# Attention beside an MLP on one core: small transfers on GpSimd's queue, the output weights' norm in the first stage, and six steps instead of four before heads' results are read

## The chip, the core and the metric

The kernel runs on one core of a Trainium2 chip. The metric is the device time of one execution in microseconds (us), the median of several runs. The engines are named as in the profile: PE (TensorE's matmuls), PEld (its weight loads), DVE (VectorE), ACT (ScalarE), POOL (GpSimd), SP (the engine that issues most transfers).

## The reference

For x of 2048 rows and 640 columns, with 32 heads of 20 columns and an MLP of width 1536:

```python
xn = _layernorm(x, axis=-1)
return x + _A_ref(xn, A_wqkv, A_wo) + _B_ref(xn, B_w1, B_b1, B_w2, B_b2)

# _A_ref(x, wqkv, wo): q, k, v = x @ wqkv, by head
scores = jnp.einsum("bhqd,bhkd->bhqk", q, k) * (Dh ** -0.5)
p = _softmax(scores, axis=-1)
o = jnp.einsum("bhqk,bhkd->bhqd", p, v)
return o (heads side by side) @ wo

# _B_ref(x, w1, b1, w2, b2)
y = _layernorm(x, axis=-1)
h = _gelu(y @ w1 + b1)
return h @ w2 + b2
```

## The kernel before

Numbers that need float32 are carried as pairs of 16-bit halves, and most products are three matmuls of halves. So that the halves keep their precision, each weight matrix is scaled by a power of two taken from its sum of squares: `squares` or a loop of ScalarE's Square activations, then `pow2` (one small matmul against ones into a PSUM tile of the tag "s", and a few VectorE operations on one column), then `split` (ScalarE scales into a tile of the tag "wtmp", VectorE casts the high half and subtracts for the low one).

**First stage (up to about 220 us).** Four chunks `c` of 512 rows. For each, `norm_a`, `norm_b` and `norm_c` make the layer norm (the reciprocal roots are powers on POOL), five steps `qk(c, tt)` make q and k for all heads, and `qk_out` stores them in DRAM (`qkscr`) in halves; then four steps `vproj(c, j)` make V, and `vproj_out` puts it in the tile `vfull`. Between these steps `some(n)` advances the generator `weights()`, which takes the sums of squares of w2 and w1 and then splits w2 (12 slices) and w1 (15 slices). PSUM has three tiles of the tag "s" in turn for qk, vproj and the norms' small matmuls. `norm_c` stores the second norm's 512 reciprocals per chunk as 4-byte elements in DRAM (`rscr`, line 272); lines 537 and 538 store a constant row and load the bias b1 (1536 elements of 4 bytes). All of these transfers are issued by SP.

**Attention (about 220 to 1281 us).** 16 pairs of heads `g`, two halves `hf` of the query rows, two column blocks `cc` and 16 key blocks `kb`, in groups of four key blocks; for the pairs below TAIL = 12 the halves alternate, after that all of half 0 comes before half 1. Each key block gives two score matmuls (`scores`, line 711), an exp on ScalarE (line 713) and, for half of the blocks, a subtraction `low` on VectorE (line 725); `pv` multiplies with V (line 742). Into these groups `other()` puts the MLP's matmuls (`layer1`, `layer2`, then `projection`) at a fixed rate. The order of everything is written out by the program: `tick()` is called twice per group and advances each side generator by one step. Generators in `sides` advance at every step; those in `patient` only in a step in which nothing else gave VectorE work, unless their last step was a mere wait.

**Finishing.** After three (later two) pairs of a half, `finish` is queued in `fins`, and one runner (`finishing`) works them off: it loads the sums of exps, takes reciprocals, stores them (`linv`), loads them back spread over the heads' rows (`rb`) and loads the two partial results (`oa` from `opart`), waits a number of steps, adds, multiplies, splits into halves and stores to `oscr` (lines 889 to 899), for 512 columns at a time. The runner was put into `sides` when it was created for half 1 at pair TAIL or later, else into `patient`.

**Output weights.** `prep_late` (line 658) starts when the MLP's first layer has ended: it loads wo over w1's place, waits four steps, squares its five slices on ScalarE one step each, takes `pow2`, and splits them on VectorE. The projection with wo comes last, half of it after attention.

Of the kernel before, what the change touches and what calls it, by code (L numbers as in the profile page):

```python
# [16 lines left out]
P = 128  # L17
# [25 lines left out]
def mha_mlp_kernel(tc, x, wqkv, wo, w1, b1, w2, b2, out):  # L43
# [4 lines left out]
    with (  # L48
# [53 lines left out]
        def pow2(acc, tag):  # L102

            lo = keep.tile([P, 1], F32, name=f"lo_{tag}")
            hi = keep.tile([P, 1], F32, name=f"hi_{tag}")
            if tag in ("q", "k"):
                pt = psM.tile([P, 512], F32, tag="m", name="mxp")
            else:
                pt = psS.tile([P, 2, 512], F32, tag="s", name="mxp")[:, 0, :]
            n = acc.shape[1]  # L110
            nc.tensor.matmul(pt[:, :n], ones, acc, start=True, stop=True)
            nc.vector.tensor_reduce(lo, pt[:, :n], AX.X, ALU.add)  # L112
# [10 lines left out]
        def split(pool, src, h, l, scale, n):  # L123

            tmp = pool.tile([P, n], F32, tag="wtmp", name="wtmp")
            nc.scalar.activation(tmp, src, AF.Copy, scale=scale)
            nc.vector.tensor_copy(h, tmp)
            nc.vector.tensor_sub(l, tmp, h)
# [33 lines left out]
        with tc.tile_pool(name="pa", bufs=2) as pa, tc.tile_pool(name="pa1", bufs=1) as pa1, tc.manual_schedule():  # L162
# [106 lines left out]
            def norm_c(c):  # L269
                mv, ve, r, r2 = rs.pop(c)  # L270
                newton(r2, ve, "b")
                nc.sync.dma_start(rscr[c * 512 : (c + 1) * 512].rearrange("(j p) -> p j", p=P), r2)

            xnts = {}

# [181 lines left out]
            def weights():  # L457

                for i in range(KF // 2):
                    if i == 0:  # L460
                        accs["2"] = sm.tile([P, 8], F32, tag="acc2", name="acc2", bufs=1)[:, : KF // 2]
                    nc.scalar.activation(junk[:, : 2 * D].rearrange("p (a b) -> p a b", a=2),
                                         w2t[:, 2 * i : 2 * i + 2, :], AF.Square, accum_out=accs["2"][:, i : i + 1])
                    yield
                scale_of("2")
                yield
                for k in range(KD):
                    if k == 0:
                        accs["1"] = sm.tile([P, 8], F32, tag="acc1", name="acc1", bufs=1)[:, :KD]
                    nc.scalar.activation(junk[:, :F], w1t[:, k, :], AF.Square, accum_out=accs["1"][:, k : k + 1])  # L470
                    yield
                scale_of("1")
                yield
                factors()
                yield
                for k in range(KF):
                    split(pa, w2t[:, k, :], w2v[:, k, 0], w2v[:, k, 1], scales["2"], D)
                    yield
                for k in range(KD):
                    for q in range(3):  # L480
                        split(pa, w1t[:, k, q * 512 : (q + 1) * 512], w1v[:, k, q, 0], w1v[:, k, q, 1], scales["1"], 512)
                        yield
# [51 lines left out]
                split_qkv("q", [k], 0, 2 * P)  # L534
            nc.sync.dma_start(xscr[:, :, :, :512], xnts[0])
            del xts[0]
            nc.sync.dma_start(bscr[H : H + 1, :].rearrange("h (r t) -> h r t", r=4), brow[0:1, None, :].to_broadcast([1, 4, S // 4]))
            nc.sync.dma_start(b1t, b1.rearrange("(k p) -> p k", p=P))
            for c in range(4):
                nxt = c + 1 if c < 3 else None  # L540
                for tt in range(5):
# [76 lines left out]
        with ExitStack() as scope:  # L618
# [36 lines left out]

            split_done = []

            def prep_late(tag, w, wv_, src, nk, slices, delay):
                nc.sync.dma_start(w, src)
                for _ in range(delay):  # L660
                    yield
                acc = sm.tile([P, 8], F32, tag="acc", name="acc")
                for i, sl in enumerate(slices):
                    junk = m1.tile([P, 2 * MC], F32, tag="u", name="junk").bitcast(BF16)[:, :D]
                    nc.scalar.activation(junk, w[:, sl, :], AF.Square, accum_out=acc[:, i : i + 1])
                    yield
                yield
                yield
                pw[tag] = pow2(acc[:, : len(slices)], tag)
                s = keep.tile([P, 1], F32, name=f"s_{tag}")  # L670
                nc.vector.tensor_scalar(s, pw[tag][1], 4096.0, None, ALU.mult)
                nc.vector.tensor_scalar(fo, pw["v"][0], 2.0**-22, pw[tag][0], ALU.mult, ALU.mult)
                yield 1.0
                for k in range(nk):
                    parts = []
                    for tag_, c0 in (("u", 0), ("w", 320)):
                        tmp = m1.tile([P, 2 * MC], F32, tag=tag_, name="wtmp")[:, :320]
                        nc.vector.tensor_scalar(tmp, w[:, k, c0 : c0 + 320], s, None, ALU.mult)
# [6 lines left out]
                split_done.append(tag)  # L685

            def project(ot, acc, t0, j):
                for hf in range(2):
# [82 lines left out]
            def unload(g, hf, ev):  # L771
                cols = slice(hf * 1024, (hf + 1) * 1024)
                direct.extend([ev] if (g, hf) == ORDER[-1] else [])
                for p in range(0 if direct else 2):
                    dma(g, hf)(lpart[p, hf, 2 * g : 2 * g + 2, :].rearrange("a (c t) -> a c t", c=2),
                                      ev[PAD + DH + VW * p :: 64])
                    for a in range(2):
                        q0, r = 64 * a + PAD + VW * p, (2 * g + a) * DH
                        dma(g, hf)(opart[p, r : r + DH, cols].rearrange("d (c t) -> d c t", c=2),
                                          ev[q0 : q0 + DH])  # L780
                if g + 1 in ENDS:
                    fins.append(finish(g + 1 - UNITS[ENDS.index(g + 1)], g + 1, hf))
                    if len(fins) == 1:

                        (sides if hf == 1 and g + 1 >= TAIL else patient).append(finishing())

            def waits(n):
                for _ in range(n - 1):
                    yield WAIT
                yield  # L790

            fins, direct = [], []
            ready = [0, 0]

            fetched = []
# [24 lines left out]
            def finish(g0, g1, hf):  # L820
# [16 lines left out]
                for c0 in range(0, 1024, w):  # L837
# [50 lines left out]
                    for h in range(0 if last else nh):  # L888
                        go(rb[h * DH : (h + 1) * DH],
                           linv[hf, 2 * g0 + h : 2 * g0 + h + 1, c0 : c0 + w].to_broadcast([DH, w]))  # L890
                    yield from waits(W2 if last else 4)
                    nc.vector.tensor_add(o0, o0, o1)
                    yield
                    nc.vector.tensor_mul(o0, o0, rb)
# [64 lines left out]
            def layer1(mc, f):  # L959
                xnt, r2f = xs[mc]  # L960
                if f == 0:
                    hTs[mc] = m0.tile([P, KF, 2, MC], F16, tag="hT", name="hT")
                ps = psM.tile([P, 2, MC], F32, tag="m", name="pu")
                for i in range(2):
                    n = 0
                    fo_ = (f + i) % 4 * P
                    for k in range(KD):
                        for a, b in PASS:
                            nc.tensor.matmul(ps[:, i], w1v[:, k, (f + i) // 4, a, fo_ : fo_ + P], xnt[:, k, b, :],  # L969
                                             start=(n == 0), stop=(n == 3 * KD - 1))  # L970
                            n += 1
                            if n % 3 == 0:
                                if i == 1 and n == 15:
                                    begin(gelu(ps, r2f, hTs[mc], f))
                                    over[0] = True
                                yield 0.3276
                if f == KF - 2:
                    if mc + 2 < NMC:
                        load_chunk(mc + 2)
                    if mc + 1 == NMC:  # L980
                        sides.append(ahead())
                        sides.append(prep_late("o", wot, wov, wo.rearrange("(k p) n -> p k n", p=P), KD,
                                               range(KD), 4))

            xbs = {}

# [292 lines left out]
```

## Time and profile before

| what | value |
|---|---|
| median of 3 runs | 1352.96 us (1352.85 to 1353.47) |
| the profiled execution's own time | 1354.35 us |
| its span, first to last instruction | 1352.6 us |
| granted TensorE clock | 0.998 |
| busy | PE 98%, ACT 83%, DVE 78%, PEld 44%, POOL 2% of the span |
| bytes moved by DMA | 127.94 MB, 95 GB/s on average |

A timeline row gives the start, the length, the engine, the line and operation, the tiles written and read, how many instructions are merged, and in brackets the idle time before it and what ended that. A row of the groups has busy time and mean length of one instruction, then the idle time before the group. In the chain of waits each piece has its start, length and what it was.

### The profile page before, as it was taken

What the parts mean: (1) busy time and instruction counts of PE and PEld (TensorE: products, weight loads), DVE (VectorE), ACT (ScalarE), POOL (GpSimd) and SP (SyncE); (2) the same over time, 40 slices, a digit from 0 to 9 for tenths busy, and PEclk for the clock granted to TensorE, in tenths of its full rate; (3) what the DMA queues carried; (4) which work ended last, traced back from release to release, by engine and by line L of the source; (5) the groups of instructions that cost most, each with busy time, mean ns of one, the idle gap of its engine ahead of it and who ended that gap; (6) DMA issues with size and microseconds to landing.
All of it is one profiled execution on the core that took longest, in us unless ns stands there. A gap on an engine that the chain in (4) does not pass through costs nothing.

```text
span 1352.6 us, 29045 instructions
## 1 busy us (share of the span) xinstructions
PE 1331.5 (98%) x11647; PEld 591.7 (44%) x11647; DVE 1056.0 (78%) x1436; ACT 1128.2 (83%) x1306; POOL 30.0 (2%) x74
## 2 busy tenths in 40 slices
PE   9999999999999999999999999999999999999997
PEld 6545545443334343434434343443433333333475
DVE  6658735998779887978897789887888898878732
ACT  7754425999999999999999999999999999999800
POOL 2000000000000000000000000000000000000000
PEclk9999999999999999999999999999999999999999
DMA  9976632121123231123321142313032323153375
GB/s 271 250 200 142 141 102 58 34 55 40 48 69 89 65 85 56 49 57 86 97 67 53 28 110 57 92 48 86 19 99 74 100 57 87 54 171 83 102 222 178
DMA packets 103217, 127.94 MB, mean 95 GB/s; under 512 B 27660, under 2 KB 69712, under 8 KB 103076
## 3 DMA queue, kind: packets, MB, share of 16 engines
q1 hardware_dynamic: 100324, 120.27, 31.6%
q0 software_dynamic: 2304, 5.24, 2.3%
q8 instruction: 93, 1.52, 0.5%
q10 hardware_dynamic: 448, 0.51, 0.2%
q14 instruction: 48, 0.39, 0.1%
HBM read 80.50 MB, written 42.51 MB: 91 GB/s over the span
## 4 chain that ended last, share of the span: by engine, by line
PE 80%; DVE 7%; ACT 6%; DMA 4%; issue 2%; SPq 1%; DVEq 0%; ACTq 0%; POOL 0%; POOLq 0%
PE o L742 25%; PE s L711 16%; PE py L1001 10%; PE pu L969 9%; PE qkp L323 8%; PE z L1080 5%; PE vp L396 5%; ACT p L713 4%; DVE low L725 3%; DMA w1t<-in_A_wo_dram 1%; DMA qkscr<-qkhl 1%; PE warm L220 1%; DMA accscr<-xb 0%; DMA oa<-opart 0%; DVE u L906 0%
## 5 line engine op out<-in xcount | busy, mean ns | idle before, releaser
L713 ACT ACTIVATE p<-s 128x1024 f32<-128x1024 f32 x1024 | 971.6, 1044 | 41.3 <-PE s L711 35.5
L725 DVE TENSOR_TENSOR low<-p 128x1024 f16<-128x1024 f32 x512 | 614.3, 1218 | 155.1 <-ACT p L713 154.8
L742 PE MATMUL o<-p,vfull 128*32 128x512 bf16 (+1 forms) x4096 | 429.7, 493 | 0.0
L711 PE MATMUL s<-qs,ks 61*128 61x512 f16 x2048 | 316.4, 381 | 8.3 <-ACT p L713 7.3
L711 PEld LDWEIGHTS <-ks 61*128 61x128 f16 x2048 | 63.6, 94 | 294.6 <-issue 291.0
L969 PE MATMUL pu<-xm,w1t 128*128 128x256 f16 x1440 | 179.3, 273 | 1.4 <-DVE u L906 1.4
L1001 PE MATMUL py<-w2t,hT 128*128 128x320 f16 x1152 | 178.4, 300 | 1.6 <-DVE u L906 1.5
L969 PEld LDWEIGHTS <-w1t 128*128 128x128 f16 x1440 | 130.6, 98 | 68.7 <-issue 55.3
L1001 PEld LDWEIGHTS <-hT 128*128 128x128 f16 x1152 | 102.6, 98 | 88.7 <-issue 54.5
L323 PE MATMUL qkp<-xnt,wv 128*128 128x512 f16 x600 | 131.1, 379 | 1.2 <-DVE lo_v L112 0.9
L742 PEld LDWEIGHTS <-vfull 128*32 128x32 f16 x3072 | 59.5, 95 | 132.4 <-issue 101.8
L742 PE MATMUL o<-low,vfull 128*32 128x512 f16 x1024 | 102.2, 378 | 0.2
L323 PEld LDWEIGHTS <-wv 128*128 128x128 f16 x600 | 58.3, 98 | 71.0 <-DVE wv L430 1.1
L742 PEld LDWEIGHTS o<-p,vfull 128*32 128x32 f32 x2048 | 62.5, 108 | 53.1
L338 ACT ACTIVATE qkhl<-qkp,qks 128x1024 f16<-128x1024 f32 (+1 forms) x24 | 23.3, 969 | 64.4 <-PE qkp L323 47.3
L396 PE MATMUL vp<-wv,xnt 128*128 128x320 f16 x480 | 66.7, 299 | 0.0
L1080 PE MATMUL z<-w1t,ot 128*128 128x320 f16 x480 | 66.3, 299 | 0.0
L339 DVE SCALAR_TENSOR_TENSOR qkhl<-qkp,qks,qkhl 128x1024 f16<-128x1024 f32 (+1 forms) x24 | 26.5, 1106 | 37.9 <-ACT qkhl L338 37.8
L1080 PEld LDWEIGHTS <-ot 128*128 128x128 f16 x480 | 46.5, 98 | 20.8 <-issue 2.9
L396 PEld LDWEIGHTS <-xnt 128*128 128x128 f16 x480 | 46.7, 98 | 18.6
L1039 DVE SCALAR_TENSOR_TENSOR acc<-z,sc,acc 128x320 f32<-128x320 f32 x32 | 17.4, 546 | 42.8 <-PE z L1080 37.0
L763 ACT ACTIVATE ev<-o 128x512 f32<-128x512 f32 x64 | 39.3, 615 | 2.5 <-PE o L742 2.5
(182 smaller groups left out, 666.6 us busy)
## 6 DMA issues: line engine op xcount, KB each, us to landing
qkscr<-qkhl SPq DMA_DIRECT2D x40, 256.0 KB
opart<-ev SPq DMA_DIRECT2D x124, 80.0 KB
ks<-qkscr SPq DMA_DIRECT2D x120, 80.0 KB
qs<-qkscr SPq DMA_DIRECT2D x192, 40.0 KB
oa<-opart SPq DMA_DIRECT2D x32, 240.0 KB
xt<-in_A_x_dram SPq DMA_DIRECT2D x16, 320.0 KB
xscr<-xnt SPq DMA_DIRECT2D x4, 1280.0 KB
xm<-xscr SPq DMA_DIRECT2D x8, 640.0 KB
```

Of the source, the lines that this page charges most:

```text
L323: nc.tensor.matmul(ps[:, i, :], wv[:, k, q, a, mm * P : (mm + 1) * P], xnts[c][:, k, b, :], start=(k + n == 0), stop=(k == KD - 1 and n == 2))
L338: nc.scalar.activation(hl[:, 0, i0:i1], ps[:, i0:i1], AF.Copy, scale=a)
L339: nc.vector.scalar_tensor_tensor(hl[:, 1, i0:i1], ps[:, i0:i1], a, hl[:, 0, i0:i1], ALU.mult, ALU.subtract)
L396: nc.tensor.matmul(ps[:, hf, :320], xnts[c][:, k, a, j * P : (j + 1) * P], wv[:, k, 2, b, hf * 320 : (hf + 1) * 320], start=(n == 0), stop ...
L711: nc.tensor.matmul(ps[:, a, :], ks[64 * a : 64 * a + 61, kb * P : (kb + 1) * P], qs[64 * a : 64 * a + 61, cc * 512 : (cc + 1) * 512], star ...
L713: nc.scalar.activation(pt, ps, AF.Exp, scale=QS)
L725: nc.vector.tensor_sub(low, pt, upper(pt))
L742: nc.tensor.matmul(pv.o[32 * q : 32 * q + 32, :], src[:, v0 - PAD * (1 - q % 2) :][:, :32], t, start=q not in pv.begun, stop=last, skip_gr ...
L763: nc.scalar.activation(evs[g, hf][:, cc], pv.o, AF.Copy)
L969: nc.tensor.matmul(ps[:, i], w1v[:, k, (f + i) // 4, a, fo_ : fo_ + P], xnt[:, k, b, :], start=(n == 0), stop=(n == 3 * KD - 1))
L1001: nc.tensor.matmul(ps[:, :320], hTs[mc][:, f, a, j * P : (j + 1) * P], w2v[:, f, b, hf * 320 : (hf + 1) * 320], start=(n == 0), stop=(n == ...
L1080: nc.tensor.matmul(ps[:, :320], ot[:, k, a, j * P : (j + 1) * P], wov[:, k, b, h * 320 : (h + 1) * 320], start=(n == 0), stop=(n == 3 * KD ...
```

## The change

The small transfers (`rscr`, the constant row of `bscr`, b1) are issued by POOL instead of SP. The sums of squares of wo are taken in the first stage: between the splits of w2, POOL loads one 128 x 640 slice at a time into a tile of the tag "wtmp" and ScalarE squares it two splits later; the scale and the output's factor `fo` are made among w1's splits. `prep_late` keeps the load of wo, now waits eight steps, and goes straight to the splits. `finish` waits six steps instead of four before adding, except for the last two units of each half, which keep four. Its runner always begins in `patient` and moves to `sides` once a half-1 unit beyond pair 12 has been queued.

```diff
@@ norm_c
-                nc.sync.dma_start(rscr[c * 512 : (c + 1) * 512].rearrange("(j p) -> p j", p=P), r2)
+                nc.gpsimd.dma_start(rscr[c * 512 : (c + 1) * 512].rearrange("(j p) -> p j", p=P), r2)
@@ weights
+                accs["o"] = sm.tile([P, 8], F32, tag="acco", name="acco", bufs=1)[:, :KD]
+                came = []
                 for k in range(KF):
+                    if k % 2 == 0 and 0 < k <= 2 * KD:
+                        nc.scalar.activation(junk[:, :D], came[-1], AF.Square, accum_out=accs["o"][:, k // 2 - 1 : k // 2])
                     split(pa, w2t[:, k, :], w2v[:, k, 0], w2v[:, k, 1], scales["2"], D)
+                    if k % 2 == 0 and len(came) < KD:
+                        came.append(pa.tile([P, D], F32, tag="wtmp", name="wos"))
+                        nc.gpsimd.dma_start(came[-1], wo[k // 2 * P : (k // 2 + 1) * P, :])
                     yield
                 for k in range(KD):
+                    if k == 1:
+                        scale_of("o")
+                        nc.vector.tensor_scalar(fo, pw["v"][0], 2.0**-22, pw["o"][0], ALU.mult, ALU.mult)
                     for q in range(3):
@@ first stage
-            nc.sync.dma_start(bscr[H : H + 1, :].rearrange("h (r t) -> h r t", r=4), brow[0:1, None, :].to_broadcast([1, 4, S // 4]))
-            nc.sync.dma_start(b1t, b1.rearrange("(k p) -> p k", p=P))
+            nc.gpsimd.dma_start(bscr[H : H + 1, :].rearrange("h (r t) -> h r t", r=4), brow[0:1, None, :].to_broadcast([1, 4, S // 4]))
+            nc.gpsimd.dma_start(b1t, b1.rearrange("(k p) -> p k", p=P))
@@ prep_late
-            def prep_late(tag, w, wv_, src, nk, slices, delay):
+            def prep_late(w, wv_, src, nk, delay):
                 nc.sync.dma_start(w, src)
-                for _ in range(delay):
-                    yield
-                acc = sm.tile([P, 8], F32, tag="acc", name="acc")
-                for i, sl in enumerate(slices):
-                    junk = m1.tile([P, 2 * MC], F32, tag="u", name="junk").bitcast(BF16)[:, :D]
-                    nc.scalar.activation(junk, w[:, sl, :], AF.Square, accum_out=acc[:, i : i + 1])
-                    yield
-                yield
-                yield
-                pw[tag] = pow2(acc[:, : len(slices)], tag)
-                s = keep.tile([P, 1], F32, name=f"s_{tag}")
-                nc.vector.tensor_scalar(s, pw[tag][1], 4096.0, None, ALU.mult)
-                nc.vector.tensor_scalar(fo, pw["v"][0], 2.0**-22, pw[tag][0], ALU.mult, ALU.mult)
-                yield 1.0
+                yield from waits(delay)
                 for k in range(nk):
...
@@ unload
                     if len(fins) == 1:
-                        (sides if hf == 1 and g + 1 >= TAIL else patient).append(finishing())
+                        patient.append(finishing())
+                        runner[:] = patient[-1:]
+                    if hf == 1 and g + 1 > TAIL and runner[0] not in sides:
+                        patient.remove(runner[0])
+                        sides.append(runner[0])
@@ finish
-                    yield from waits(W2 if last else 4)
+                    yield from waits(W2 if last else 4 if g1 > TAIL else 6)
@@ layer1
-                        sides.append(prep_late("o", wot, wov, wo.rearrange("(k p) n -> p k n", p=P), KD,
-                                               range(KD), 4))
+                        sides.append(prep_late(wot, wov, wo.rearrange("(k p) n -> p k n", p=P), KD, 8))
```

More of the change, by code (lines that the diff above doesn't have):

```diff
@@ L677, in prep_late @@
                         tmp = m1.tile([P, 2 * MC], F32, tag=tag_, name="wtmp")[:, :320]
-                        nc.vector.tensor_scalar(tmp, w[:, k, c0 : c0 + 320], s, None, ALU.mult)
+                        nc.vector.tensor_scalar(tmp, w[:, k, c0 : c0 + 320], scales["o"], None, ALU.mult)
                         parts.append((tmp, slice(c0, c0 + 320)))
@@ L684, in prep_late @@
                         yield 0.7
-                split_done.append(tag)
+                split_done.append(1)
             def project(ot, acc, t0, j):
@@ L790, in waits @@
                 yield
-            fins, direct = [], []
+            fins, direct, runner = [], [], []
             ready = [0, 0]
```

## The prediction

> **What bounds the kernel now.** I read the page's totals first, then a table of 30 us stretches, and then the rows of TensorE's timeline that show a pause.
>
> ```profile
> PE 1331.5 (98%) x11647; PEld 591.7 (44%) x11647; DVE 1056.0 (78%) x1436; ACT 1128.2 (83%) x1306; POOL 30.0 (2%) x74
> L713 ACT ACTIVATE p<-s 128x1024 f32<-128x1024 f32 x1024 | 971.6, 1044 | 41.3 <-PE s L711 35.5
> L725 DVE TENSOR_TENSOR low<-p 128x1024 f16<-128x1024 f32 x512 | 614.3, 1218 | 155.1 <-ACT p L713 154.8
> 1060.00:1090.00 30.00, 28.21 (x269) 11.55 (x267) 26.80 (x33) 27.84 (x33) 0.85 (x1) 1.00 0.35 91
> 1090.00:1120.00 30.00, 29.17 (x270) 11.73 (x270) 26.34 (x35) 28.37 (x33) 0.00 (x0) 1.00 0.19 52
> 1150.00:1180.00 30.00, 29.91 (x286) 11.78 (x287) 23.69 (x31) 29.23 (x34) 0.00 (x0) 1.00 0.19 56
> 1210.00:1240.00 30.00, 27.03 (x238) 10.42 (x234) 20.07 (x36) 28.66 (x38) 0.00 (x0) 1.00 0.32 99
> ```
>
> In a stretch row the columns after the length are busy us (and instructions) of PE, its weight loads, DVE, ACT and POOL, then clock, DMA share and GB/s. TensorE is busy 98% of the span at full clock. ScalarE's exps wait 41.3 us, 35.5 of them for TensorE's scores: TensorE leads, ScalarE is close behind (29.23 of 30 us in the stretch from 1150). A queue that is always full ends earlier only if it gets less work or fewer pauses. In both built kernels the matmuls, apart from the norms' small ones, stand in one and the same order, so this change can act only through pauses. The 512 `low` subtractions span some 1060 us of attention, so one step of the step counter is about 2.07 us. These are the pauses the change can touch:
>
> ```profile
> 43.94 6.65 PE L323 MATMUL qkp<-xnt,wv 128*128 128x512 f16 x30 [0.88 <-DVE lo_v L112]
> 435.57 1.52 PE L1001 MATMUL py<-w2t,hT 128*128 128x320 f16 x10 [0.65 <-DVE u L906]
> 1077.57 1.14 PE L969 MATMUL pu<-xm,w1t 128*128 128x256 f16 x9 [1.42 <-DVE u L906]
> 1090.48 1.79 PE L1001 MATMUL py<-w2t,hT 128*128 128x320 f16 x12 [0.55 <-DVE u L906]
> 1216.91 0.39 PE L711 MATMUL s<-qs,ks 61*128 61x512 f16 x2 [1.96 <-ACT p L713]
> ```
>
> **Part 1: the norm of wo leaves attention.** Five squares, each with its read of the sum, ran on ScalarE beside the exps, behind a load of 12.27 us:
>
> ```profile
> 1202.34 12.27 DMA w1t<-in_A_wo_dram
> L665 ACT ACTIVATE junk<-w1t 128x640 bf16<-128x640 f32 x5 | 3.8, 765 | 0.7 <-DMA w1t<-in_A_wo_dram 0.7
> L665 ACT ACTIVATION_READ_ACCUMULATOR junk<-w1t 128x1 f32 x5 | 1.1, 226 | 0.0
> L111 PE MATMUL mxp<-acc,ones 128*128 128x5 f32 (+3 forms) x14 | 2.3, 233 | 0.1
> ```
>
> That is 3.8 + 1.1 + 0.7 = 5.6 us on an engine with at most 1 us to spare in 30. TensorE lost 30 - 27.03 = 2.97 us in that stretch, 1.96 in the one pause at 1216.91. A stretch of the same phase without the squares (from 1150) loses 0.09. I take 2.6 of the 2.97 as gained and leave 0.4 for the ten splits of wo on VectorE, which now begin some five steps earlier beside the same finishing work. If all of the cover were an illusion (VectorE late instead), the gain is the squares' alone, 1.96; the ends are 1.9 and 2.97. The larger delay, 8 steps or about 16.5 us against the load's 12.27, keeps VectorE from meeting an unlanded wo. The two small matmuls of the norm (233 ns each) are paid in either place: zero.
>
> **Part 2: six steps for the heads' results.** The finishing step waits a fixed number of steps, then adds on VectorE; if the load has not landed, VectorE's whole queue (`low`, the MLP's `u`) stands behind it.
>
> ```profile
> 484.92 0.69 DVE L892 TENSOR_TENSOR oa<-oa 120x512 f32<-120x512 f32 x1 [1.03 <-DMA oa<-opart]
> 1072.04 0.69 DVE L892 TENSOR_TENSOR oa<-oa 120x512 f32<-120x512 f32 x1 [1.26 <-DMA oa<-opart]
> 1192.25 0.69 DVE L892 TENSOR_TENSOR oa<-oa 80x512 f32<-80x512 f32 x1 [1.25 <-DMA qs<-qkscr]
> ```
>
> Two more steps are 4.1 us, over three times each wait. The wait at 1072 is followed by TensorE's 1.42 at 1077.57: gained. The one at 484.92 left no pause, so it is worth nothing. The one at 1192 belongs to the tail groups, which keep four steps. The finishing that caused 1072 also stops being pushed ahead of the MLP's VectorE work (it is now `patient`): its last addition stands after the 430th `low`, not the 413th. The same 16 operations per finishing are issued, only later; the projection's first block still waits for a finishing that ends after the 503rd `low` in both orders. All of these insertions shift against the MLP's, so the pauses of 0.65 and 0.55 may vanish or similar ones appear: 0 taken, +/- 1.2 kept. Gain 1.4, ends 0 and 2.6.
>
> **Part 3: small elements leave SP's queue.** The pause at 43.94 goes back to a store that landed late:
>
> ```profile
> 25.61 2.96 SPq L272 DMA_DIRECT2D rscr<-r  x1
> 28.66 11.75 DMA qkscr<-qkhl
> 25.00:30.00 5.00, 5.00 (x27) 2.38 (x25) 3.39 (x14) 4.97 (x11) 0.00 (x0) 1.00 0.99 271
> 30.00:35.00 5.00, 5.00 (x25) 2.29 (x24) 4.67 (x8) 5.00 (x7) 0.00 (x0) 1.00 1.30 61
> 35.00:40.00 5.00, 5.00 (x25) 2.26 (x24) 4.81 (x12) 4.26 (x6) 0.00 (x0) 1.00 0.99 85
> 40.90 0.69 ACT L338 ACTIVATE qkhl<-qkp,qks 128x512 f16<-128x512 f32 x1 [1.58 <-DVE ve L243]
> ```
>
> The engines stay full (1.30, 0.99) while the rate falls from 271 to 61 and 85 GB/s, right after the transfers of 4-byte elements. The third `qkhl` needs the first one's buffer, whose store runs from 28.66 to 40.41; ScalarE idles 1.58. On POOL's queue the bias goes out near the start and the `rscr` store no longer stands in line behind `xscr`. If the `qkscr` store lands 1.1 us earlier or more, the 0.88 go. A clear queue gives 0.88, an unchanged landing 0; I take 0.6. The Trainium skill ("DMA: Bandwidth & Descriptors", section "Issuing engines are not separate DMA queues") says that transfers from all queues run on the same 16 engines and interleave. By that the slow writes stay and this term is 0, the sum 0.6 less. This trace has no such store from POOL, so it cannot decide.
>
> The price is at the start, where the q loads set the pace, and POOL is free from 7.7 us:
>
> ```profile
> 7.22 0.51 POOL L213 MEMSET brow<- 32x512 f16 x1
> 23.75 1.04 POOL L267 TENSOR_TENSOR r<-ve,nhalf 128x4 f32<-128x4 f32 x1 [16.01 <-DVE ve L266]
> 12.68 0.74 ACT L514 ACTIVATE junk<-w1t 128x640 bf16<-128x640 f32 x1
> 13.33 0.19 ACT L514 ACTIVATION_READ_ACCUMULATOR junk<-w1t 128x1 f32 x1
> 14.04 0.28 PE L111 MATMUL mxp<-acc,ones 128*128 128x5 f32 x2
> ```
>
> The squares of q run back to back until 13.52, the matmul that needs them starts at 14.04: 0.5 us of slack. The bias's 1536 elements then compete with the last q loads. I put 0.2 on it (ends 0 and 1.0). Behind them on POOL stands the power of norm 0, which VectorE releases only at 23.75 us: POOL may be busy with the small elements until then at no cost.
>
> **Part 4: the norm of wo enters the first stage.** Five loads of 320 KB from POOL, five squares on ScalarE. The loads use the same two buffers as the splits' `wtmp`, so a split waits for VectorE to finish the one before, and a square for a load issued only after that.
>
> ```profile
> L126 ACT ACTIVATE wtmp<-w2t,s 128x640 f32<-128x640 f32 x12 | 9.9, 825 | 4.3 <-DVE w2t L128 4.3
> L128 DVE TENSOR_TENSOR w2t<-wtmp,w2t 128x640 f16<-128x640 f32 x12 | 9.9, 826 | 0.4
> L127 DVE CAST w2t<-wtmp 128x640 f16<-128x640 f32 x12 | 5.8, 485 | 0.0
> L406 ACT ACTIVATE vfull<-vp 128x640 f16<-128x640 f32 (+1 forms) x16 | 11.2, 698 | 21.6 <-PE vp L396 20.0 <-remote 1.5
> xb<-in_B_b_dram POOLq DMA_DIRECT2D x16, 320.0 KB, 4.4
> L991 POOL DMA_DIRECT2D xb<-in_B_b_dram x16 | 14.0, 874 | 1022.4 <-DMA xb<-in_A_x_dram 492.7 <-DMA ks<-bscr 168.5 <-DVE oa L894 119.1
> 111.87 8.32 PE L396 MATMUL vp<-wv,xnt 128*128 128x320 f16 x60
> 105.00:115.00 10.00, 10.00 (x95) 7.05 (x94) 9.79 (x18) 5.36 (x8) 0.00 (x0) 1.00 0.97 159
> 115.15 0.82 DVE L408 SCALAR_TENSOR_TENSOR vfull<-vp,vfull 128x640 f16<-128x640 f32 x1
> 120.03 10.31 PE L323 MATMUL qkp<-xnt,wv 128*128 128x512 f16 x47
> ```
>
> Follow one square: `vfull` 0.70, a split 0.83, VectorE's cast and subtraction 1.31, the load L, the square 0.99, another split 0.83, and the `vfull` two blocks of V later. Two blocks therefore need 4.66 + L; TensorE's two take 8.32. With POOL's own median of 4.4 us from issue to landing that is 9.06, some 0.4 us behind per block, 1.5 after four. The room is larger: the block written at 115.15 to 115.97 is overwritten from 120.03, 4.06 us later. So no pause, up to L of about 5.7. VectorE gets seven operations more for the scale, and the norm's PSUM tile takes one of three from the blocks around 153 us; for that I charge 0.3 (ends 0 and 2).
>
> A rule that speaks against it: the Trainium skill ("SBUF — State Buffer", section "SBUF: two separate sides") says that VectorE in a two-port mode locks GpSimd out, so that it cannot write its descriptors. The row of 16 POOL issues beside a VectorE that is 78% busy shows 874 ns each and no such hold; by the rule L would be longer, which is the second rival.
>
> **The sum**, against the profiled execution's own time of 1354.35 us (span 1352.6 and 1.75 around it): -2.6 - 1.4 - 0.6 + 0.2 + 0.3 = -4.1, so 1350.25. That execution lies 1.39 above the median of the runs, 1352.96; on the runs' scale this is **1348.9 us**. A measurement of this kernel can tell about 0.2%, 2.7 us, from no change: faster means under 1350.3, slower over 1355.7.
>
> **The rivals.** *Half of it (27%):* TensorE is bound, but the finishing's new places make as many pauses as they remove, and the slow small writes stay slow on the shared engines. Left is part 1 alone, 1.9 to 2.6, against 0.5 of costs: about 1351.1, no change by the bound. The pauses of 0.2 to 0.65 all over attention speak for it, the size of 1077.57 against. *The norm's loads come late (16%):* they share engines that are 97% busy at 159 GB/s from 105 to 115 us, with transposes, x loads and a slow `rscr` store; the whole wo took 12.27 in attention. At L = 10 two blocks take 14.7, so 3.2 us is lost per block, 12.7 after four, less the 4.06 of room: a pause of 8.7 us around 120 to 140 us, 1357.6, slower. It decides from L = 5.7; at L = 8 it costs 4.7 and eats the whole gain. The median of 4.4 speaks against, the load on the engines there for it. *More than that (7%):* the pauses of 0.65 and 0.55 go too and every term reaches its end: 1346.8.
>
> **How the numbers follow.** My forecast has 50%. Faster: 50 + 7 = 57%. Half of it, and late loads of the cheaper kind (3 of the 16), make 30% of no change. Slower 13%. The range runs from 1346.9 to 1354.5: it holds the forecast, the half and the cheap late loads, and leaves out the costly ones and half of the last case. The forecast's own range is 1347.4 to 1350.2.
>
> **What would show it.** Right: the pause at 1216.91 gone and the stretch there above 29 us of TensorE; no wait of `oa` for its loads before the tail; TensorE going on near 43.1 instead of 43.94; squares of `wos` waiting for their loads a few us in sum, and no pause of TensorE between 100 and 160 us over 0.5. Wrong: the matmul of q's norm later than 14.04; `wos` loads landing over 6 us after issue and TensorE waiting for `vfull` or `qkhl`; new pauses of over 1 us behind `u` in attention.

## The result, and the profile after

In the first timing the changed kernel took **1349.37 us** (median of 11 runs, 1348.39 to 1350.66) against 1352.85 for the kernel before (11 runs, 1351.68 to 1355.86): ratio 0.9979, interval 0.9971 to 0.9986. That is 0.5 us over the forecast of 1348.9. In the last set of experiments, where it was timed again, the same file took 1353.73 against 1354.20: ratio 0.9996, interval 0.9985 to 1.0007. Both results have to be explained, and they come from different places in the kernel.

First the profile from the first timing (1349.61 us, span 1347.7). From the page and a table of stretches, the rows that answer to those of before:

```profile
PE 1330.8 (99%) x11647; PEld 590.7 (44%) x11647; DVE 1055.8 (78%) x1436; ACT 1128.6 (84%) x1306; POOL 37.9 (3%) x85
L711 ACT ACTIVATE p<-s 128x1024 f32<-128x1024 f32 x1024 | 971.4, 1042 | 41.2 <-PE s L709 35.4
1060.00:1090.00 30.00, 29.52 (x282) 12.18 (x278) 27.57 (x34) 28.22 (x33) 0.84 (x1) 1.00 0.25 64
1150.00:1180.00 30.00, 30.00 (x287) 11.82 (x288) 25.45 (x33) 29.24 (x34) 0.00 (x0) 1.00 0.22 67
1210.00:1240.00 30.00, 28.37 (x252) 10.65 (x252) 25.21 (x44) 26.61 (x30) 0.00 (x0) 1.00 0.43 127
```

Work and rates are as they were; TensorE only stands still less. The stretch from 1060 rose from 28.21 to 29.52 us of TensorE, the one from 1210 only from 27.03 to 28.37, less than the "above 29" that I had asked for.

Since the matmuls keep their order, the same matmul can be found in both timelines, and the difference of its two start times is what has been gained up to there. TensorE's rows, before:

```profile
237.06 0.39 PE L711 MATMUL s<-qs,ks 61*128 61x512 f16 x2 [0.23 <-ACT p L713]
1027.41 0.39 PE L711 MATMUL s<-qs,ks 61*128 61x512 f16 x2 [0.20 <-ACT p L713]
1116.42 0.39 PE L711 MATMUL s<-qs,ks 61*128 61x512 f16 x2 [0.35 <-ACT p L713]
1198.57 0.39 PE L711 MATMUL s<-qs,ks 61*128 61x512 f16 x2 [0.35 <-ACT p L713]
1251.96 0.39 PE L711 MATMUL s<-qs,ks 61*128 61x512 f16 x2 [0.47 <-ACT p L713]
1277.39 0.60 PE L711 MATMUL s<-qs,ks 61*128 61x512 f16 x4
```

and the same six in the changed kernel:

```profile
236.11 0.39 PE L709 MATMUL s<-qs,ks 61*128 61x512 f16 x2 [0.23 <-ACT p L711]
1025.56 0.39 PE L709 MATMUL s<-qs,ks 61*128 61x512 f16 x2 [0.20 <-ACT p L711]
1112.94 0.39 PE L709 MATMUL s<-qs,ks 61*128 61x512 f16 x2 [0.35 <-ACT p L711]
1195.09 0.39 PE L709 MATMUL s<-qs,ks 61*128 61x512 f16 x2 [0.34 <-ACT p L711]
1246.89 0.39 PE L709 MATMUL s<-qs,ks 61*128 61x512 f16 x2 [0.47 <-ACT p L711]
1272.61 0.61 PE L709 MATMUL s<-qs,ks 61*128 61x512 f16 x4
```

The shifts are -0.95 early in attention, -1.85 at 1027, -3.48 at 1116 and at 1198, -5.07 at 1252 and, behind one more pause of the changed kernel, -4.78 at the last scores. So 0.95 comes from the first stage, 0.90 from the long middle, 1.63 from around 1077, nothing from 1116 to 1198, and 1.30 from the stretch where wo's norm had stood. I had taken 2.6 for that last one. In that stretch TensorE has these pauses in the changed kernel:

```profile
1228.84 0.39 PE L709 MATMUL s<-qs,ks 61*128 61x512 f16 x2 [0.38 <-ACT p L711]
1232.58 2.06 PE L1002 MATMUL py<-w2t,hT 128*128 128x320 f16 x14 [0.57 <-DVE xb L936]
1249.84 2.06 PE L1002 MATMUL py<-w2t,hT 128*128 128x320 f16 x14 [0.38 <-DVE xb L936]
```

and ahead of them stands a wait that the kernel before did not have. SP's queue and VectorE, changed kernel:

```profile
1199.93 0.41 SPq L670 DMA_DIRECT2D w1t<-in_A_wo_dram  x1
1213.78 0.34 SPq L901 DMA_DIRECT2D oscr<-oa  x1
1215.04 0.96 SPq L1034 DMA_DIRECT2D ot<-oscr  x2
1216.10 0.47 SPq L1035 DMA_DIRECT2D acc<-accscr  x1
1216.61 1.14 SPq L833 DMA_DIRECT2D lt<-lpart  x2
1224.31 0.22 DVE L870 TENSOR_TENSOR lt<-lt 64x64 f32<-64x64 f32 x1 [2.19 <-DMA lt<-lpart]
```

and SP's queue in the kernel before:

```profile
1199.99 0.34 SPq L899 DMA_DIRECT2D oscr<-oa  x1
1200.37 1.07 SPq L1033 DMA_DIRECT2D ot<-oscr  x2
1219.46 1.13 SPq L831 DMA_DIRECT2D lt<-lpart  x2
```

`ot` and `acc` are piece 0 of the projection. `ahead()` loads it once the first half's last unit is finished, that is, right behind that unit's last store (`oscr`). With six steps that unit ends later, so piece 0 is asked for at 1215.04 and not at 1200.37. It now stands right ahead of the small `lt` loads; VectorE waits 2.19 us for them with its whole queue behind it. My theory was that this wait, brought by the six steps, spent part of what the norm's removal had won.

### The profile page after: what moved, and what is told of

Its sections match the earlier page's. It is cut to its first block, busy times and chain, and to the rows that moved or that the text cites. A ratio compares the mean times of both kernels' runs of the same rounds, so it can differ in the third digit from the quotient of the medians.

```text
span 1347.7 us, 29060 instructions
## 1 busy us (share of the span) xinstructions
PE 1330.8 (99%) x11647; PEld 590.7 (44%) x11647; DVE 1055.8 (78%) x1436; ACT 1128.6 (84%) x1306; POOL 37.9 (3%) x85
## 4 chain that ended last, share of the span: by engine, by line
PE 83%; DVE 8%; ACT 4%; issue 2%; DMA 1%; SPq 1%; DVEq 0%; POOL 0%; ACTq 0%; POOLq 0%
PE o L740 26%; PE s L709 16%; PE py L1002 11%; PE qkp L323 10%; PE pu L971 9%; PE z L1081 5%; PE vp L396 5%; DVE low L723 4%; ACT p L711 3%; PE warm L220 1%; DMA lt<-lpart 1%; DVE u L908 0%; ACT ev L761 0%; DVE u L918 0%; DVE u L910 0%
## 5 line engine op out<-in xcount | busy, mean ns | idle before, releaser
L992 POOL DMA_DIRECT2D xb<-in_B_b_dram x16 | 13.8, 863 | 1018.7 <-DMA xb<-in_A_x_dram 624.8
```

## The experiments

The kernels ran in three sets, each set on a chip of its own. The spread of whole runs (up to 6 us within a kernel) is as large as the parts looked for, so the profiles carry the argument. One profile was taken of each version in each set. This table holds, for every profile, TensorE's pauses in us: near 43 in the first stage; behind `vfull` or `qkhl` from 115 to 160; behind `u` near 435 and near 1077; and its idle time from 1180 to 1270 (90 less the busy time).

| kernel | 43 | 115-160 | 435 | 1077 | 1180-1270 |
|---|---|---|---|---|---|
| before | 0.88 | 0 | 0.65 | 1.42 | 3.86 |
| before_again | 2.30 | 0 | 0.68 | 1.06 | 4.06 |
| queue_only | 0 | 0 | 0.67 | 0 | 3.34 |
| rscr0_alone | 0.31 | 0 | 0.69 | 0 | 4.29 |
| six_only | 1.79 | 0 | 0 | 0 | 3.40 |
| norm_only | 2.43 | 0 | 0.68 | 1.59 | 1.72 |
| changed kernel | 0 | 0 | 0 | 0 | 2.81 |
| after_again | 0 | 0 | 0 | 0 | 2.81 |
| after_timed | 0 | 3.86 | 0 | 0 | 2.56 |
| piece_later | 0 | 1.66 | 0 | 0 | 1.72 |
| rscr_first_only | 0 | 0 | 0 | 0 | 1.72 |
| rscr_first_timed | 1.25 | 1.71 | 0 | 0 | 1.72 |
| eight_steps | 0 | 1.54 | 0 | 0 | 1.72 |
| no_wo_norm | 0 | 0 | 0 | 0 | 1.72 |

(In queue_only and before_again TensorE ran a few us of the last stretch at half clock, so their 3.34 and 4.06 can't be set beside the others; the third set comes back to this. The time of before_again, with a mean granted clock of 0.996, isn't used.)

**First set: each part alone, and the new wait taken away.** The kernel before took 1354.08 on this chip.

*queue_only:*

```diff
-nc.sync.dma_start(rscr[...], r2)
+nc.gpsimd.dma_start(rscr[...], r2)      # likewise the bscr row and b1t
```

> The kernel before with one of the parts alone: its small transfers (the squared reciprocals to rscr, the bound's row to bscr, b1t) on POOL's queue, nothing else. Theory (SP's queue held up the first qk store): the pause of 0.88 us at 43.94 goes, the tensor engine begins the attention about 0.95 us earlier than before (237.06 to about 236.1), every later pause of before (435.57, 1077.57, 1216.91) stays where it is, and the time falls by 0.9 us. Rival (the transfers meet on the same DMA engines whichever queue issues them): the pause stays near 43 to 44 and the time stays within 0.3 us. Rival (the gain at the start came from the chip's run, not from the queue): the start of the attention is not earlier than 236.9.

Measured: 1352.00, ratio 0.9985 (0.9976 to 0.9995). The pause near 43 is gone and the first scores start 1.28 us earlier than before, so the first theory holds for the start; the median fell by 2.1 us, not 0.9. Two things were not expected: the pause near 1077 is gone too, without the six steps; and ScalarE waits 5.71 us for a transposing load:

```profile
1069.29 0.68 DVE L892 TENSOR_TENSOR oa<-oa 120x512 f32<-120x512 f32 x1
108.83 0.74 ACT L304 ACTIVATE row<-xt 128x640 f16<-128x640 f32 x1 [5.71 <-DMA xnt<-row]
```

The first row is the addition that had waited 1.26 us at 1072.04. Here its load was issued at 1063.83 and was there in time, 5.5 us later; before, it was issued at 1066.05 and used 6.0 us later. Four steps are just about what the landing takes. So the 1.4 us at 1077 can go with the queue alone, too: by start times queue_only gains 1.35 there.

*six_only:* the runner that changes lists, and

```diff
-yield from waits(W2 if last else 4)
+yield from waits(W2 if last else 4 if g1 > TAIL else 6)
```

> The kernel before with the six steps (and the runner that changes lists with them) alone. Theory: the pauses <-DVE u at 435.57 (0.65) and at 1077.57 (1.42) both hang on the finishing's adds, so both go and the time falls by 2.1 to 2.6 us; the finishing of the first half's last unit ends later, so the load of piece 0 goes right ahead of the lt loads and VectorE waits about 2 us for lt near 1220 to 1230, which the late norm of wo in that stretch hides or doesn't (up to 0.5 us back). Rival: the pause at 435 has another cause and stays: 1.4 us. Rival: what is won is spent again behind later adds that now meet loaded stretches: under 0.5 us.

Measured: 1352.12, ratio 0.9987 (0.9979 to 0.9996). Both pauses behind `u` are gone; the profile gains 1.0 around 435 and 1.6 around 1077. Piece 0 moved to 1217.04, and VectorE waited 0.95 for `lt`. The theory holds for the pauses, and both rivals fall; the median fell by 1.96 us, just under the 2.1 of the theory.

*norm_only:* the changed kernel with SP's queue and four steps put back.

> The kernel before with wo's norm between the splits alone (finishing with four steps, small transfers on SP). Theory (part of the norm's gain was spent on a new wait that the six steps brought: piece 0 loaded ahead of lt): here piece 0 is asked for near 1200 as before, VectorE doesn't wait for lt, the tensor engine's idle time from 1180 to 1270 falls from 3.87 us to 1.6 or less, and the time falls by 2.3 to 2.6 us. Rival (VectorE is simply full there, with wo's splits beside the finishing): the idle time stays near 2.8 us without any wait for lt, and the time falls by 1.1 to 1.6 us.

Measured: 1352.04, ratio 0.9987 (0.9978 to 0.9995). The stretch from 1180 to 1270, in the order norm_only, changed kernel, piece_later:

```profile
1180.00:1270.00 90.00, 88.28 (x806) 33.75 (x808) 78.37 (x109) 84.69 (x95) 1.84 (x2) 1.00 0.39 115
1180.00:1270.00 90.00, 87.19 (x799) 32.82 (x791) 76.16 (x108) 83.09 (x92) 1.70 (x2) 1.00 0.43 128
1180.00:1270.00 90.00, 88.28 (x811) 33.03 (x809) 77.88 (x110) 84.63 (x94) 1.90 (x2) 1.00 0.44 129
```

Piece 0 was asked for at 1203.02, `lt` met no wait, and the idle time fell to 1.72, just over the 1.6 of the theory; the median fell by 2.04 us, between the theory's 2.3 and the rival's 1.6. A fixed window holds other matmuls in each kernel, so I take the same two score matmuls instead, those at 1198.57 and 1277.39 before. They are 78.82 us apart there, 75.76 in norm_only, 77.52 in the changed kernel and 75.78 in piece_later. The norm alone wins 3.06 us; in the changed kernel, beside the new wait, 1.30. So the loss is the six steps' doing and not that of a full VectorE, which was busy 78.37 us here against 76.16.

*piece_later:*

```diff
 while ready[0] < len(UNITS) or not done[0]:
     yield
+yield from waits(4)
 load_piece(0)
```

> The changed kernel, with the load of piece 0 four steps later, so that the lt and oa loads of the last unit stand ahead of it on SP's queue. Theory (the wait for lt is what spent part of the norm's gain): the wait of 2.19 us of VectorE for lt goes, the tensor engine's idle time from 1180 to 1270 falls from 2.82 us to about 1.5, and the time is 1.0 to 1.5 us under the changed kernel's (1348.1, some 4.7 under before). Rival (VectorE is full there whatever lt does): the idle time stays over 2.4 us and the time within 0.4 us of the changed kernel's 1349.4.

Measured: 1349.07 (6 runs), ratio 0.9969 (0.9957 to 0.9981). SP's queue and VectorE:

```profile
1216.61 1.14 SPq L833 DMA_DIRECT2D lt<-lpart  x2
1223.29 0.96 SPq L1034 DMA_DIRECT2D ot<-oscr  x2
1223.47 0.21 DVE L870 TENSOR_TENSOR lt<-lt 64x64 f32<-64x64 f32 x1
```

With the order of the two loads turned round the wait is gone and the idle time is 1.72 again. The mechanism is shown; by the start times above it costs 1.74 us (77.52 less 75.78; 1.1 by the idle time of the window). The other four rows of the table that have the same edit, the last four, show the same 1.72. The median lies 5.0 us under this chip's kernel before, where 4.7 was expected, but it didn't come down to the 1348.1; this profile has a pause of 1.66 at 120.32 that the changed kernel's first profile has not. The second set goes after it.

**Second set: landings in the first stage.** The kernel before took 1352.24 here.

*rscr_first_only:* piece_later, and the later chunks' reciprocals back on SP.

```diff
-nc.gpsimd.dma_start(rscr[...], r2)
+(nc.gpsimd if c == 0 else nc.sync).dma_start(rscr[...], r2)
```

> The kernel with the later load of piece 0, with the squared reciprocals of the first chunk alone on POOL's queue and those of chunks 1 to 3 back on SP's. Theory (on POOL the third chunk's reciprocals, issued near 95, delay the transposing loads behind them, and row waits for these: 0.81, 4.52 and 5.71 us in the three runs with all four on POOL, none in the three with all on SP): the wait of row near 104 to 109 goes, no pause of the tensor engine near 120 comes, the attention begins near 236, and the median is 0.3 to 1.0 us under 1349.1. Rival (the wait of row is the landing's own spread and belongs to no queue): row waits again by 1 us or more and the median stays within 0.3 us of 1349.1. Rival (the third chunk's reciprocals on SP hold up a qk store there): a pause of 0.5 us or more comes between 95 and 130.

Measured: 1348.07 (6 runs, 1347.89 to 1348.24), ratio 0.9968 (0.9956 to 0.9980). As the theory expected: no wait of `row`, no pause, and the score matmul of 237.06 at 236.03. It did not hold up in the third set, see below.

*rscr0_alone:* the kernel before with only the first chunk's reciprocals moved.

> The kernel before with nothing but the first chunk's reciprocals on POOL's queue; the bound's row and b1t stay on SP. Theory (the 512 elements of 4 bytes are what held up the first qk store on SP): the pause near 43 to 45 (0.88, 1.79 and 2.43 us in the three runs with the reciprocals on SP) is gone or under 0.2. Rival (b1t's 1536 elements at 8 us are what delays the stores): the pause stays at 0.8 us or more.

Measured, one run: 1352.45; the pause near 43 is 0.31, between the two theories' marks. By this one profile the reciprocals are the greater part of it; whether the remaining 0.31 belong to the bias and its row or to the spread is open.

*before_again:* nothing changed.

> The kernel before, unchanged, for a second profile of it. Theory (the pauses that hang on a landing spread from run to run, those that hang on the order of the instructions don't): the pause at 435.57 (0.65), that at 1216.91 (1.96) and the seventeen of 0.20 to 0.47 behind p come again within 0.1 us, while the pause near 43 to 45 lies anywhere from 0.5 to 2.5 us and that near 1077 anywhere from 0 to 1.6. Rival: all come again within 0.1 us, and the differences seen belong to the changes.

*after_again:* nothing changed.

> The changed kernel, unchanged, for a second profile of it. Theory (order brings the lt wait, landings bring the start's spread): VectorE waits 0.9 us or more for lt near 1224 and the tensor engine's idle time from 1180 to 1270 is again 2.4 to 3.0 us; the pauses near 43 and near 1077 are absent again; a pause near 120 of 0 to 1.7 us may come, according to how long row and wos wait. Rival: lt does not wait here, and the idle time of that stretch falls to 1.7 or less.

Measured: 1359.09 and 1349.53, one run each. In before_again the pause at 435 came again at 0.68, those near 43 and 1077 at 2.30 and 1.06; the one at 1216.91 was 2.79, not 1.96, so there the theory's 0.1 fails: this pause comes every time but spreads (2.04 in queue_only, 2.37 in rscr0_alone). In after_again `lt` waits 2.18 and the stretch loses 2.81. So the pause of 435 and the presence of the `lt` wait hang on order (its length spreads, 1.32 in after_timed); those of 43 and 1077 hang on landings.

**Third set: the changed kernel again.** The kernel before took 1354.20.

*after_timed* (the changed kernel) and *rscr_first_timed* (the file of rscr_first_only):

> The changed kernel, unchanged, timed beside the next one on the same chip. Theory (one wait for lt and one for row are all that the two later edits take away): its median lies 0.8 to 1.8 us over the next kernel's. Rival (what those waits cost comes back elsewhere in the runs that aren't profiled): the two medians lie within 0.4 us.

> The changed kernel with the later load of piece 0 and with only the first chunk's reciprocals on POOL, timed again beside the changed kernel. Theory: 1348.1, and 0.8 to 1.8 us under the changed kernel of the same chip; the tensor engine idles at most 1.8 us from 1180 to 1270. Rival: within 0.4 us of it.

Measured: 1353.73, ratio 0.9996 (0.9985 to 1.0007), and 1351.21, ratio 0.9977 (0.9966 to 0.9989), so 2.5 us between them where 0.8 to 1.8 was expected, and 1351.21 where 1348.1 was. ScalarE and TensorE of after_timed:

```profile
111.75 0.74 ACT L304 ACTIVATE row<-xt 128x640 f16<-128x640 f32 x1 [8.54 <-DMA xnt<-row]
119.34 0.74 ACT L481 ACTIVATE junk<-wos 128x640 bf16<-128x640 f32 x1 [2.24 <-DMA wos<-in_A_wo_dram]
116.97 4.23 PE L396 MATMUL vp<-wv,xnt 128*128 128x320 f16 x30 [1.84 <-DVE vfull L408]
123.22 27.76 PE L323 MATMUL qkp<-xnt,wv 128*128 128x512 f16 x120 [2.02 <-DVE vfull L408]
124.00:127.00 3.00, 3.00 (x9) 1.07 (x8) 0.72 (x1) 1.26 (x3) 0.13 (x1) 0.50 1.02 377
```

and of rscr_first_timed:

```profile
109.99 0.74 ACT L304 ACTIVATE row<-xt 128x640 f16<-128x640 f32 x1 [5.36 <-DMA xnt<-row]
121.83 26.07 PE L323 MATMUL qkp<-xnt,wv 128*128 128x512 f16 x120 [1.41 <-DVE vfull L408]
```

Here is where the gain went in that profile: TensorE waits 3.86 us in the first stage for `vfull`, behind a ScalarE that waits for transposes and for `wos`. The 120 matmuls also took 27.76 us in place of 26.07, 1.7 more, because the granted clock was 0.50 from 124 to 127 us, right behind the pause of 2.02. Together that is 5.6 us, about what this span (1353.2) has over that of the changed kernel's first profile (1347.7).

The half clock looks like the pause's doing. In the first stage and attention of the fourteen profiles TensorE has six pauses over 2.0 us. Within 1 us of the end of five of them (2.02 here, 2.04 in queue_only, 2.30 and 2.79 in before_again, 2.43 in norm_only) a stretch of half clock begins, 3.4 to 6.9 us long; the sixth, 2.37 in rscr0_alone, has none. Behind no pause of 1.96 or less does one come there. (After attention there is one more, in eight_steps at 1286.6, behind a pause of 0.55.) No run was made to test this.

And `row` waited 5.36 us with the third chunk's reciprocals on SP: my theory that this wait belongs to the reciprocals on POOL's queue falls. It came in all five profiles with those reciprocals on POOL (0.81 to 8.54 us), in two of four with them on SP and `wos` between the splits, and in none of the five with neither. So transfers from POOL at that place, of either kind, stay under suspicion; how they make the transposing load late isn't shown.

ScalarE's waits for `row` and `wos` up to the pause, against the pause:

| kernel | waits | pause there |
|---|---|---|
| changed kernel | 0.81 + 1.99 | 0 |
| norm_only | 2.88 | 0 |
| rscr_first_only | 3.12 | 0 |
| after_again | 2.81 + 2.35 | 0 |
| eight_steps | 4.43 + 2.64 | 0.50 |
| rscr_first_timed | 5.36 + 2.62 | 1.41 |
| piece_later | 4.52 + 0.28 + 3.33 | 1.66 |
| after_timed | 8.54 + 2.24 | 1.84 + 2.02 |

Up to 5.2 us the waits cost nothing; from 7.07 on the pause is their sum less some 6.5, within 0.5. I read this as the room that the first stage has up to about 120 us; it is fitted to four profiles, not tested. Waits behind that place don't count: the changed kernel has two more there, 4.11 and 0.41, and no pause. (queue_only waited 5.71 for `row` without a pause. The 1.04 and 0.30 that eight_steps and rscr_first_timed lose near 154 behind `qkhl` are not in this count.)

*eight_steps:*

```diff
-4 if g1 > TAIL else 6
+4 if g1 > TAIL else 8
```

> The kernel of the run before with eight steps in place of six in the finishing. Theory (six is enough for the landing, and what is left are the places among the MLP's VectorE work): no wait of VectorE for oa or rb before the tail, as with six; the pauses behind u (0.32 near 827, 0.28 near 1087) move or change by at most 0.7 us in sum either way, and the time stays within 0.7 us of the run before. Rival (more time to land is worth more, since some landings were still late): 0.8 us or more faster. Rival (the finishing then runs into the next unit's, or its last part falls among the projection's splits): slower by 1 us or more, with pauses behind xb or low from 1180 to 1270.

Measured: 1349.72, ratio 0.9968 (0.9957 to 0.9979), 1.5 us under rscr_first_timed. By the median that is the first rival's 0.8 or more, and not the theory's 0.7. But in the profiles TensorE gained 0.6 us over six steps from the first scores to 1277, and 1.6 in the first stage, whose order is the same in both. So some 0.6 is what the steps can be seen to give, and which of the two is right stays open.

*no_wo_norm:* wo's loads and squares taken out, w1's sums of squares in their place.

> The kernel with the later load of piece 0 and the first chunk's reciprocals alone on POOL, but without wo's loads and squares between the splits: wo's own norm is left out and the norm of w1 stands in its place. It tells what the fourth part of the change costs at the start. Theory (its price is in the idle time of ScalarE and VectorE, not in the tensor engine's): the stretch from the 120 matmuls near 69 to the first scores at 236 is at most 0.2 us shorter, though ScalarE no longer waits 3 to 7 us for wos. Rival (it takes the tensor engine's time in all runs, as in the one with the pause of 1.66 near 120): that stretch is 0.5 us shorter or more.

Measured, one run: 1347.83. The score matmul that stood at 237.06:

```profile
236.02 0.39 PE L703 MATMUL s<-qs,ks 61*128 61x512 f16 x2 [0.22 <-ACT p L705]
```

From the 120 matmuls near 69 (68.81) this is 167.21 us, against 167.20 in rscr_first_only (68.83 to 236.03). So where the loads land in time, the fourth part costs TensorE nothing. No profile without `wos` between the splits had a pause from 115 to 160 (six profiles); four of the eight with it did.

The version of rscr_first_only, the piece later and the first reciprocals alone on POOL, beat the kernel before in both sets (by 0.2 to 0.3%) and the changed kernel in the set where both were timed; in the other it took 1348.07 beside after_again's single 1349.53. With eight steps it was not slower.

## Why the prediction was right or wrong, point by point

**What bounds the kernel: right.** TensorE's pauses account for most of what moved, 4.1 of the 4.8 us up to the last scores; the rest lies in matmuls that took a little less time and wasn't followed up. No other engine's work took TensorE's place.

**Part 1, the norm leaves attention: the term was mis-sized, 2.6 against 1.30.** The pause of 1.96 went as said, and the ten splits cost little: alone, with four steps, the norm's removal moved the later matmuls by 3.06 us. The step that failed stands in part 2: "the projection's first block still waits for a finishing that ends after the 503rd `low` in both orders". That is the wrong finishing: the one at the 503rd `low` works for the second half. The first block and the load of piece 0 wait for the first half's last unit (`ready[0]`), whose last operation on VectorE stands behind the 474th `low` before and behind the 482nd now. The block itself didn't mind, as its first matmul stands behind the 506th `low` in both kernels. But the *load* is released by that unit's end, went out some fifteen microseconds later (1215.04 for 1200.37) and came in front of `lt`; the wait cost 1.74 us. I had not asked who is released by a finishing's end.

**Part 2, six steps: right in place, too small, and partly a matter of landing.** The 1.42 at 1077 went (1.4 taken, 1.63 measured). The reason given, the landing, fits: with four steps the pause came in three of five profiles, with six or more in none of nine, six_only among them. But the three have the first reciprocals on SP and the two without the pause have them on POOL. Whether that is chance, or the queue moves this landing, is open, and so is how the 1.63 divides between parts 2 and 3. The 0.65 at 435, for which I had taken 0 with 1.2 either way, goes whenever the finishing is at its new place and never otherwise; with the smaller pauses around it that is 0.90 more.

**Part 3, the queue: right in direction, 0.6 against 0.95.** Over all runs it is worth more than the profile of before showed: that pause was 0.88 to 2.43 in the four profiles with the first reciprocals on SP, and 0 in eight of the ten with them on POOL (0.31 and 1.25 in the others). Behind the two longest, 2.30 and 2.43, the next 30 matmuls ran 1.6 to 1.7 us longer, at half clock. In the changed kernel, ScalarE's third `qkhl`, which had idled 1.58, and the stretches behind the reciprocals:

```profile
39.17 0.67 ACT L338 ACTIVATE qkhl<-qkp,qks 128x512 f16<-128x512 f32 x1
30.00:35.00 5.00, 5.00 (x25) 2.24 (x23) 4.61 (x8) 5.00 (x7) 0.00 (x0) 1.00 0.53 60
35.00:40.00 5.00, 5.00 (x25) 2.25 (x23) 4.86 (x12) 4.78 (x6) 0.00 (x0) 1.00 0.68 217
```

The 60 GB/s from 30 to 35 are as slow as the 61 of before, which agrees with the rule of the Trainium skill ("DMA: Bandwidth & Descriptors", section "Issuing engines are not separate DMA queues") that transfers interleave on the same engines whoever issues them. But from 35 to 40 the rate is 217 instead of 85, and the store that was waited for is there. The term of 0 that I had worked out by that rule didn't come. The price at the start, 0.2, was 0: the matmul behind q's squares starts at 13.97, not later than 14.04.

**Part 4, the norm in the first stage: the forecast held in the changed kernel's first profile, the rival came in four later ones.** The rows of `wos` in the changed kernel:

```profile
113.40 0.74 ACT L481 ACTIVATE junk<-wos 128x640 bf16<-128x640 f32 x1 [1.99 <-DMA wos<-in_A_wo_dram]
121.51 0.74 ACT L481 ACTIVATE junk<-wos 128x640 bf16<-128x640 f32 x1 [4.11 <-DMA wos<-in_A_wo_dram]
```

Their loads were issued at 110.18 and 113.43, so they were there 3.2 and 8.1 us later. The second is over the 5.7 from which I let the rival "the norm's loads come late" decide, and TensorE didn't pause. The point was put at the wrong place: one late load doesn't decide, the sum of ScalarE's waits up to about 120 us seems to, with a room of about 6.5 us, and in the four profiles with a pause the larger summand is a wait that I hadn't counted, that of `row` for its transposing load. At 16% with 4.7 to 8.7 us the rival was put rarer and dearer than it was: pauses in four of eight profiles, of 1.5 to 3.9 us, and 1.7 of half clock behind the longest.

By the other rule (the Trainium skill, "SBUF — State Buffer", section "SBUF: two separate sides") POOL's issues should have been held up whenever VectorE ran in a two-port mode. The five of `wos` took 599 ns in the mean, less than the 874 of the 16 loads of `xb`: no such hold in the issues themselves; why some loads land after 3 us and others after 8 is open.

**The sum: right by errors that cancel.** By place, profile against profile: -1.30 for -2.6; -2.53 (0.90 and 1.63) for -1.4; -0.95 for -0.4, the first stage's terms together (-0.6 + 0.2); and nothing for the +0.3. Together -4.78 instead of -4.1, of which the median shows 3.5, since the profiled execution of before lay 1.5 above the median of its 11 runs and that of the changed kernel 0.2. That the forecast came within 0.5 us is luck in this sense, and so is the first timing: in the last set the same file took 1353.73, outside the forecast's own range of 1347.4 to 1350.2.

## What to carry to other kernels

When a step is moved later, follow what *starts* on its completion, not only what reads its result: here a prefetch released 15 us later stepped in front of a small load that a whole engine's queue was waiting for, and more than half the gain of another edit went with it (1.74 of 3.06); four steps' delay of the prefetch brought it back. In a stage full of transfers, add up the waits of the engine in the middle against the room of the one that bounds, over several executions: one profile without a pause doesn't say that the loads fit. And where a change is the sum of parts of 1 to 2 us, run the parts alone and compare the same instruction's start in both timelines; medians of runs that spread by 3 us can't tell them apart.

## What was not expected of the hardware

The landing of one and the same transfer spreads by several us from execution to execution: `row`'s transposing load cost a wait of 0.81, 2.81 and 8.54 us in three profiles of the changed kernel, and a `wos` load of 320 KB was there after 3.2 us and after 8.1 in one profile. The sets differed too: over its runs the changed kernel took 1348.4 to 1350.7 in the first timing and 1352.0 to 1357.9 in the last, where the kernel before took 1351.7 to 1355.9 and 1351.5 to 1357.6. Taking 512 four-byte elements off SP shortened that queue's issue from 2.96 us there to 0.82 on POOL, and the rate still fell to 60 GB/s behind them. And five of the six pauses of TensorE of 2.0 to 2.8 us were followed by 3.4 us or more at half clock; in the first stage the matmuls behind them took 1.6 to 1.7 us longer for it.
